# The written orders of a gated linear attention with an FFN behind it, laid out anew on all five queues of one core

## The chip, the cores and the metric

The kernel runs on one core of one Trainium2 chip. The core has a matrix engine (TensorE, PE in the rows of the profile), a vector engine (VectorE, DVE), an activation engine (ScalarE, ACT), a general engine (GpSimd, POOL) and a queue that issues transfers (SyncE, SP). Each takes its own instructions in the order in which they were written, and they meet only at semaphores. The metric is the time of one execution on the device in microseconds (us). The kernel before has a median of 187.74 us over three runs (187.13 to 188.03).

## The reference

Attention first: 4 batches, 8 heads, 768 steps, 48 channels a head, with a state of 48 x 48 for each head that decays by a gate for each channel.

```
f = 1 / (1 + exp(-f_logit))
for t in range(S):
    state = f[t][:, None] * state + outer(k[t], v[t])
    y[t]  = q[t] @ state
x   = y as 3072 tokens x 384
out = (relu(x @ w_gate) * (x @ w_val)) @ w_out        # 384 -> 1536 -> 384, float32
```

## The kernel before, in words

**Chunks.** The 768 steps are worked in windows of 128. A *unit* is two windows of one batch; there are 12 units (`seq`): units 0 to 3 are the first 256 steps of the four batches, 4 to 7 the next, 8 to 11 the last. The window w of unit u is 2u or 2u + 1. Each SBUF row holds two neighbouring steps (an even and an odd one).

**What a unit does** (`unit`, L525). It loads f, k, q and v (L468, 384 KB each, from SP). ACT makes `exp(-f)` (L546) and its logarithm `ln(1 + ..)`, into `bneg` in units 0 to 2 (L555), or in place with a sum of the two steps on another engine (L552, "sum") in the units behind. PE makes the running sums over a window with a triangular matrix (L562 to L564, into a PSUM bank called bc). ACT takes the exponentials of these with either sign (L577, L580, L587): `expo` in SBUF or in place in the bank. DVE and POOL multiply q and k by them: the *hats* (L599 for whole ones, L605 for halves). Units 0 to 3 transpose the hats on PE (L637, with a copy to `qkT`, L402 on ACT or L403 on DVE), the others by a transfer that SP issues (L648). PE multiplies k and q for the scores (L662); the causal mask is laid on by DVE straight from PSUM (L676) or by a copy on ACT (L671) and a product on POOL (L673): `ptm`. v is copied to `vpad` and `vrest` in pieces (L400, L402, L403). The decay of a window, `dec`, comes from a small matmul (L699, L703) and an exponential (L708), or from a row of `expo` by way of DRAM (`rates`, L683 and L692). PE sums k times v into a state (L717, L727); `new_state` (L506) adds the old state (`ssum`, L517, DVE) and multiplies by the decay (L520, POOL; L513 for the first). `out_of` (L740) makes a window's output from scores times v and q times the old state, transposed in place (L760) or plain (L767, L771) with a transposing transfer behind it (L790), into `xT`.

**The FFN.** Four windows make a group of 512 tokens, six groups. `ffn_hidden` (L799) does one of twelve slices of 128 hidden channels: three matmuls for the gate and three for the value (L811), a relu on ACT (L816), their product on DVE (L823, `gT`). Groups 0 and 1 work the first six slices in two halves of 256 tokens. `ffn_out` (L829) makes a window's output in four steps of three matmuls (L841), then a copy (L402 or L403, `osb`) and a store (L862).

**Weights.** POOL issues twelve transfers (L482), four slices of each matrix, which also convert to bf16. In POOL's queue they stand between its other work. Two of the loads are named as things that a slice must wait for, in the string `FIRST`.

**What sets the order.** Everything is recorded first as 1,088 operations with a running number, and the order on each engine is a written list of these numbers, `SEQUENCE` (from L184). `HOMES` says which PSUM tile lives in which of the eight banks, and in which order; a tile waits until the one before it in its bank has been read. `UNITS` names the engine for each copy, hat, mask product and sum (k0 is the hat of k at the even steps, tk the copy of k's transposes, m01 a mask product, v10 a piece of v, r0 and r1 its rest, x0 and o0 the copies of outputs). `FILLERS` puts matmuls on zeros (L892) ahead of some operations of PE at the start: after the first of its waits and before the others. `follow` (L85) takes the lists as they are, `needs` (L131) finds which semaphores an instruction has to wait for, and `run` (L904) writes each engine's stream. The estimated durations in the code choose nothing any more.

Some numbers that the text below uses: loads 37 to 40 are f, k, q, v of unit 0, 41 to 44 those of unit 1. On ACT 65, 66 are the exponential and the logarithm of unit 0, 103 and 104 those of unit 1, 69, 70, 73, 74 the exponentials of unit 0's sums. On POOL 53 to 60 are the slices wg0, wv0, wg1, wv1, wg2, wv2, wg3, wv3. On PE 154 is the first projection, 184 and 188 values of the second weight slice, 570 the running sum of unit 6. 588 and 589 are the transposing transfers of unit 6, 647 the rates of unit 7.

## Time and profile before

| | |
|---|---|
| median of three runs | 187.74 us (187.13 to 188.03) |
| profiled execution | 187.22 us, its span 186.0 us |
| TensorE busy | 179.1 us (96%) |
| VectorE, ScalarE, GpSimd busy | 123.1, 119.9, 103.4 us |
| data moved | 32.89 MB, mean 177 GB/s |

In the page, a line of the groups names the source line, the engine, the operation, the tiles as out<-in and the shapes, then the busy time and the mean duration of one, then the idle time ahead of it and what ended that. A line of the timeline begins with the start in us from the span's start and the length; "x3" is three instructions in a row, and what stands in square brackets is idle time ahead and what ended it. Matmuls overlap each other, so a row of PE shows a longer time than the pitch at which they follow. A line of the chain is a piece of the work that ended last. In the rows of the stages stand the stretch, its length, and for PE, weight loads, DVE, ACT and POOL the busy time and number of instructions, then the granted clock, the share of the DMA engines and GB/s. "DMA to landing" gives the shortest, the median and the longest time from the issue of a transfer to its landing, for the transfers asked for. "PEld" is the loading of weights into TensorE, which lies beside the matmuls; "SPq" and "POOLq" are the queues in which transfers are issued.

### The profile page before, as it was taken

How to read it: one execution, taken by the hardware profiler on the slowest of the kernel's cores; microseconds unless marked ns; L12 is line 12 of the kernel's file. 1: busy time of each engine (PE TensorE's matmuls, PEld its weight loads, DVE VectorE, ACT ScalarE, POOL GpSimd, SP SyncE). 2: the span in 40 equal slices, each digit the busy share in tenths (PEclk: the TensorE clock that was granted, in tenths of full speed). 3: DMA queues.
4: the chain of work that ended last, by engine and by line, in shares of the span. 5: the costliest groups of instructions: out<-in, count | busy, mean ns of one | idle time of the engine just before them, and what ended most of it. 6: DMA issues, size and time to landing. Idle time of an engine off the chain costs nothing.

```text
span 186.0 us, 4305 instructions
## 1 busy us (share of the span) xinstructions
PE 179.1 (96%) x1672; PEld 103.7 (56%) x1694; DVE 123.1 (66%) x235; ACT 119.9 (64%) x242; POOL 103.4 (56%) x137
## 2 busy tenths in 40 slices
PE   7888899999999999999999999999999999999995
PEld 2455486467577555545655554556545465445464
DVE  4289866799278989789669777785785352252531
ACT  3989796958987887988776563653664640444302
POOL 5179944999356789989829987540850550000000
DMA  5999999959899999899998898988034332110105
GB/s 152 325 325 285 231 204 206 266 96 175 173 305 180 238 314 263 206 186 217 251 243 214 237 227 194 201 135 226 4 74 124 97 85 76 42 46 0 42 0 212
DMA packets 83167, 32.89 MB, mean 177 GB/s; under 512 B 75334, under 2 KB 83148, under 8 KB 83148
## 3 DMA queue, kind: packets, MB, share of 16 engines
q1 hardware_dynamic: 78348, 29.09, 64.1%
q0 software_dynamic: 4800, 3.54, 12.7%
q8 instruction: 13, 0.21, 0.4%
q14 instruction: 6, 0.05, 0.1%
HBM read 25.96 MB, written 4.73 MB: 165 GB/s over the span
## 4 chain that ended last, share of the span: by engine, by line
PE 75%; POOL 7%; DMA 6%; SPq 4%; ACT 3%; DVE 2%; issue 2%; POOLq 0%; DVEq 0%
PE ps L811 44%; PE ps L841 21%; DMA q_in<-in_q_dram 6%; SPq L468 4%; PE ps L662 2%; POOL hats L605 2%; PE ps L771 1%; PE ps L637 1%; PE ps L760 1%; POOL ptm L673 1%; PE ps L767 1%; POOL hats L599 1%; POOL vpad L403 1%; POOL st L520 1%; PE ps L727 1%
## 5 line engine op out<-in xcount | busy, mean ns | idle before, releaser
L823 DVE TENSOR_TENSOR gT<-relu,ps 128x512 bf16<-128x512 bf16 (+1 forms) x84 | 49.7, 625 | 29.9 <-PE ps L811 28.7
L816 ACT ACTIVATE relu<-ps 128x512 bf16<-128x512 f32 (+1 forms) x84 | 43.1, 536 | 32.5 <-PE ps L811 21.6
L811 PE MATMUL ps<-xT,wg 128*128 128x512 bf16 (+1 forms) x242 | 53.9, 348 | 0.9 <-issue 0.3
L811 PE MATMUL ps<-xT,wv 128*128 128x512 bf16 (+1 forms) x243 | 53.6, 348 | 0.5 <-issue 0.2
L841 PE MATMUL ps<-wo,gT 128*128 128x384 bf16 (+2 forms) x300 | 52.2, 320 | 0.0
L841 PEld LDWEIGHTS ps<-wo,gT 128*128 128x128 bf16 x300 | 28.3, 98 | 18.5 <-ACT ptm L671 0.2
L811 PEld LDWEIGHTS ps<-xT,wg 128*128 128x128 bf16 x252 | 23.5, 98 | 20.1 <-DVE hats L599 0.4
L605 POOL TENSOR_TENSOR hats<-q_in,expo 64x384 bf16<-64x384 f32 x28 | 27.9, 995 | 11.7 <-ACT expo L580 8.3
L811 PEld LDWEIGHTS ps<-xT,wv 128*128 128x128 bf16 x252 | 23.4, 98 | 19.2 <-DVE gT L823 0.4
L673 POOL TENSOR_TENSOR ptm<-ptm,seen 128x512 bf16<-128x512 bf16 x21 | 23.9, 1156 | 16.3 <-ACT ptm L671 16.1
L605 DVE TENSOR_TENSOR hats<-k_in,ps 64x384 bf16<-64x384 f32 x32 | 17.6, 551 | 5.8 <-ACT osb L402 2.4
L676 DVE TENSOR_TENSOR ptm<-ps,seen 128x512 bf16<-128x512 f32 x27 | 17.5, 685 | 3.2 <-PE ps L662 3.0
L671 ACT ACTIVATE ptm<-ps 128x512 bf16<-128x512 f32 x21 | 12.1, 608 | 7.4 <-PE ps L662 7.2
L520 POOL TENSOR_TENSOR st<-ssum,dec 128x384 bf16<-128x384 f32 x16 | 13.2, 830 | 3.3 <-DVE ssum L517 2.4
L402 ACT ACTIVATE osb<-ps 128x384 f32<-128x384 f32 x17 | 8.3, 487 | 6.7 <-PE ps L841 5.0
L580 ACT ACTIVATE expo<-ps 128x384 f32<-128x384 f32 x22 | 10.2, 496 | 2.6 <-DVE ps L569 2.6
L403 POOL CAST vpad<-v_in 64x384 bf16<-64x384 f32 x22 | 11.0, 500 | 1.3
L546 ACT ACTIVATE f_in<-f_in 128x768 f32<-128x768 f32 x12 | 10.1, 846 | 2.4 <-DMA f_in<-in_f_logit_dram 2.3
L517 DVE TENSOR_TENSOR ssum<-ps,st 128x384 f32<-128x384 f32 x16 | 8.8, 554 | 4.0 <-PE ps L717 2.9
L552 POOL TENSOR_TENSOR bneg<-f_in 128x384 bf16<-128x384 f32 x8 | 8.0, 995 | 5.9 <-ACT f_in L550 5.7
L587 ACT ACTIVATE ps<-ps 128x384 f32<-128x384 f32 x22 | 10.6, 494 | 0.0
L892 PE MATMUL ps<-zeros 128*128 128x512 bf16 (+4 forms) x26 | 8.2, 448 | 0.3 <-DVE ptm L676 0.2
(90 smaller groups left out, 172.8 us busy)
## 6 DMA issues: line engine op xcount, KB each, us to landing
f_in<-in_f_logit_dram SPq DMA_DIRECT2D x12, 384.0 KB, 4.5
v_in<-in_v_dram SPq DMA_DIRECT2D x12, 384.0 KB, 4.9
k_in<-in_k_dram SPq DMA_DIRECT2D x12, 384.0 KB, 5.8
q_in<-in_q_dram SPq DMA_DIRECT2D x12, 384.0 KB, 5.0
out_dram<-osb SPq DMA_DIRECT2D x22, 192.0 KB, 2.1
wg<-in_moe_w_gate_dram POOLq DMA_DIRECT2D x4, 288.0 KB, 8.1
wv<-in_moe_w_val_dram POOLq DMA_DIRECT2D x4, 288.0 KB, 9.7
wo<-in_moe_w_out_dram POOLq DMA_DIRECT2D x4, 288.0 KB, 6.0
```

Of the source, the lines that this page charges most:

```text
L403: return engine[e].tensor_copy(out, src)
L520: add(e, lambda: engine[e].tensor_tensor(t4(s_new), t4(tmp), rate, ALU.mult), [key] + dk, [f"S{b}_{y}"], **(dict(occ=0.79, lat=0.1) if e = ...
L580: add("ACT", lambda: sc.activation(expo[:, ei, i, 0, :], bc[i].ap[:, 0:HD], AF.Exp, scale=-1.0), [bc[i]], [f"expq{ei}_{i}"], **act_t(HD))
L587: add("ACT", lambda i=i, ex=ex: sc.activation(bc[i].ap[:, 0:HD] if in_place else ex[:, 1, :], bc[i].ap[:, 0:HD], AF.Exp, scale=1.0), [bc[i ...
L605: op = add(e, lambda i=i, n=n, x=x, e=e, y=y, lo=lo, exps=exps: engine[e].tensor_tensor(hats[64 * i:64 * i + 64, hi, y, x, :, 0:D], by_i[n ...
L671: add("ACT", lambda pt=pt, s=sj[j]: sc.activation(pt, s.ap[:, :].rearrange("p (n t) -> p n t", n=NP), AF.Copy), [sj[j]], [f"raw{mis[y]}_{j ...
L673: add("POOL", lambda pt=pt, mask=mask: gp.tensor_tensor(pt, pt, mask, ALU.mult), [f"raw{mis[y]}_{j}", "seen"], [f"raw{mis[y]}_{j}", f"ptm{ ...
L676: add("DVE", lambda pt=pt, mask=mask, s=sj[j]: ve.tensor_tensor(pt, s.ap[:, :].rearrange("p (n t) -> p n t", n=NP), mask, ALU.mult), [sj[j ...
L811: mm = te.matmul(bank.ap[:, 0:n], wt[:, kt, j * 128:(j + 1) * 128], xT[xi][:, kt, n0:n1], start=(kt == 0), stop=(kt == NK - 1))
L816: add("ACT", lambda: sc.activation(relu[ri][:, n0:n1], gate.ap[:, 0:n], AF.Relu), [gate], rk, **act_t(n))
L823: return ve.tensor_tensor(o, a, b, ALU.mult)
L841: mm = te.matmul(bank.ap[:, 0:cut[1] - cut[0]], gT[gi][:, j, r * C:(r + 1) * C], wo[:, j, cut[0]:cut[1]], start=(j == 0), stop=(j == NJ - 1))
```

## The change

All operations stay as they are, with the same numbers. What changes is the five lists in `SEQUENCE`, the banks in `HOMES`, the places of the fillers, the engines of 65 operations in `UNITS`, and the loads that the weight slices wait for in `FIRST`. In SP's list unit 0's q becomes the third load and v of unit 1 the ninth. In ACT's list the four exponentials of unit 0's sums (74, 70, 69, 73) stand ahead of unit 1's logarithm (104). Of unit 0, the even hat of k goes to POOL and the odd one to DVE, and the copy of k's transposes from ACT to DVE. The profile's line numbers of the kernel after are larger by one from `FILLERS` on.

```diff
 SEQUENCE = {
     "PE": [
-        36, 68, 67, 132, 106, 105, 93, 83, 85, 90, 121, 87, 123, 95, 96, 125, 128, 99, 244, 135, 134, 245, 138, 154, 146, 178, 174, 150, 170,
...
+        36, 68, 67, 85, 106, 83, 105, 87, 123, 90, 121, 132, 128, 125, 93, 244, 95, 134, 96, 99, 245, 135, 138, 154, 146, 150, 174, 262, 170,
+        148, 152, 172, 178, 156, 176, 260, 180, 190, 186, 182, 166, 184, 162, 164, 158, 168, 268, 264, 188, 160, 198, 273, 192, 202, 194, 290,
...
     "ACT": [
-        65, 66, 103, 104, 69, 73, 74, 70, 94, 10, 133, 107, 108, 111, 112, 84, 81, 79, 80, 78, 124, 242, 243, 97, 130, 120, 246, 247, 100, 250,
...
+        65, 66, 103, 74, 70, 69, 73, 104, 10, 111, 78, 107, 108, 112, 124, 242, 116, 243, 133, 79, 115, 130, 94, 246, 247, 97, 100, 250, 136,
...
     "DVE": [
-        22, 17, 18, 14, 19, 15, 16, 28, 24, 26, 25, 2, 23, 11, 12, 13, 5, 117, 71, 27, 72, 76, 86, 113, 109, 92, 122, 91, 89, 88, 98, 101, 127,
...
+        22, 11, 27, 23, 14, 26, 25, 24, 15, 12, 17, 2, 18, 5, 76, 72, 28, 75, 86, 84, 82, 89, 113, 13, 109, 19, 88, 92, 16, 122, 91, 129, 127,
...
     "POOL": [
-        30, 33, 6, 20, 21, 8, 3, 9, 32, 35, 34, 4, 0, 1, 7, 75, 110, 53, 116, 31, 77, 114, 82, 118, 54, 119, 55, 115, 56, 131, 57, 58, 102, 141,
...
+        0, 30, 8, 33, 31, 6, 9, 7, 20, 21, 1, 3, 4, 71, 114, 110, 53, 80, 32, 77, 54, 117, 81, 120, 118, 119, 55, 131, 56, 57, 58, 141, 59, 34,
...
     "SP": [
-        37, 41, 44, 38, 39, 43, 42, 40, 45, 47, 46, 49, 48, 50, 51, 52, 142, 283, 323, 143, 144, 145, 284, 285, 425, 424, 286, 329, 471, 470,
...
+        37, 41, 39, 38, 43, 40, 42, 45, 44, 47, 46, 49, 48, 50, 51, 52, 283, 142, 323, 143, 144, 284, 285, 286, 145, 424, 425, 329, 445, 471,
...
-FILLERS = {68: (9, 0, 448), 132: (3, 0, 256), 83: (2, 0, 320), 85: (1, 0, 0), 90: (5, 0, 384), 123: (1, 0, 0), 96: (2, 0, 0), 134: (2, 6, 0)}
+FILLERS = {68: (9, 0, 448), 85: (6, 0, 192), 106: (0, 0, 512), 87: (2, 0, 0), 123: (4, 1, 384), 132: (1, 1, 0), 128: (1, 2, 0), 95: (1, 0, 0)}
...
-FIRST = 'f0 k0 q0 v0 f1 k1 q1 v1 f2 k2 q2 v2 f3 k3 q3 v3 wg0@q0 wv0 wg1 wv1@f1 wg2@k0 wv2@k2 wg3@q1 wv3 wo0@k3 wo1@q0 wo2@q1 wo3'
+FIRST = 'f0 k0 q0 v0 f1 k1 q1 v1 f2 k2 q2 v2 f3 k3 q3 v3 wg0@f0 wv0@f1 wg1@f0 wv1@k1 wg2@k0 wv2@k0 wg3@v1 wv3@f0 wo0@v0 wo1@k2 wo2@f2 wo3@q3'
```

The banks and engines follow in the same way: `HOMES` has eight new rows, and in `UNITS` for instance unit 0 goes from `'tk': 'ACT', 'r1': 'ACT', 'v11': 'POOL', 'v10': 'ACT', 'k0': 'DVE', 'k1': 'POOL'` to `'tk': 'DVE', 'r1': 'POOL', 'v11': 'DVE1', 'v10': 'POOL', 'k0': 'POOL', 'k1': 'DVE'`.

More of the change, by code (lines that the diff above doesn't have):

```diff
@@ new lines @@
+    7: {'v10': 'POOL', 'kps': True, 'q1': 'POOL', 'v01': 'ACT', 'q11': 'POOL', 'm00': 'DVE', 'v11': 'ACT', 'even': 'DVE', 'm10': 'POOL', 'm11': 'DVE', 'm01': 'POOL', 'q10': 'POOL', 'qps': False, 'q01': 'POOL', 'q0': 'POOL', 'o0': 'ACT', 'x1': 'DVE', 'td': True, 'x0': 'ACT', 'o1': 'ACT', 'v00': 'POOL', 'sum': 'POOL'},
+    8: {'m10': 'DVE', 'v11': 'ACT', 'q01': 'POOL', 'm01': 'POOL', 'even': 'DVE', 'q0': 'POOL', 'v10': 'DVE1', 'q1': 'POOL', 'm00': 'DVE', 'kps': True, 'q11': 'POOL', 'q00': 'POOL', 'qps': False, 'v00': 'DVE1', 'q10': 'POOL', 'v01': 'ACT', 'pr': False, 'td': True, 'x0': 'ACT', 'o1': 'DVE', 'x1': 'DVE', 'o0': 'ACT', 'sum': 'POOL'},
@@ L274 @@
+    11: {'q0': 'DVE', 'v01': 'ACT', 'q10': 'POOL', 'm00': 'DVE', 'q01': 'POOL', 'm11': 'POOL', 'q1': 'POOL', 'q00': 'POOL', 'kps': True, 'v11': 'POOL', 'm01': 'DVE', 'q11': 'POOL', 'even': 'DVE', 'v00': 'POOL', 'm10': 'POOL', 'v10': 'ACT', 'yy': True, 'o1': 'DVE', 'td': True, 'x0': 'ACT', 'x1': 'ACT', 'o0': 'DVE', 'sum': 'DVE'},
 }
 SLICES = {'wg': [3, 3, 3, 3], 'wv': [3, 3, 3, 3], 'wo': [3, 3, 3, 3]}
[L276 removed]
+FIRST = 'f0 k0 q0 v0 f1 k1 q1 v1 f2 k2 q2 v2 f3 k3 q3 v3 wg0@f0 wv0@f1 wg1@f0 wv1@k1 wg2@k0 wv2@k0 wg3@v1 wv3@f0 wo0@v0 wo1@k2 wo2@f2 wo3@q3'
```

46 lines of the change are left out of this document (21 added, 25 removed), and 81 rows, old and new, of tables (SEQUENCE, UNITS).

## The prediction

> **What bounds the kernel now.** I read the page's busy shares and slices first, then the stages, then TensorE's own waits, and last the chain.
>
> ```profile
> PE 179.1 (96%) x1672; PEld 103.7 (56%) x1694; DVE 123.1 (66%) x235; ACT 119.9 (64%) x242; POOL 103.4 (56%) x137
> ...
> PE   7888899999999999999999999999999999999995
> ...
> DMA  5999999959899999899998898988034332110105
> ```
> ```profile
> 20.00:40.00 20.00, 19.55 (x241) 13.03 (x246) 15.01 (x32) 14.84 (x35) 14.32 (x19) 1.00 1.10 209
> ...
> 60.00:80.00 20.00, 19.74 (x249) 11.20 (x251) 17.50 (x33) 17.18 (x35) 17.78 (x21) 1.00 1.03 253
> ```
> ```profile
> PE ps L811 <- issue: 0.5, 3, 0.2
> PE ps L811 <- DVE ssum L517: 0.2, 1, 0.2
> ```
> The last two rows are all the waits of TensorE (PE) between 24 and 184 us: 0.7 us in 160. From 24 us on the kernel is a gapless stream of matmuls, so a new order cannot make that part shorter by more than 0.7 us; it can only put holes into it. What can be gained lies ahead of 24 us, where units 0 and 1 run as a chain over all engines:
>
> ```profile
> 4.42 4.84 DMA q_in<-in_q_dram
> ...
> 15.28 1.02 ACT qkT L402
> ...
> 18.87 0.53 ACT vpad L402
> ...
> 20.00 0.57 DVE st L513
> ...
> 20.86 0.55 PE ps L760 x25
> 21.41 2.42 PE ps L811 x18
> ...
> 24.73 2.29 PE ps L811 x21
> ...
> 176.71 7.36 PE ps L841 x57
> ...
> 184.09 0.29 DVE osb L403
> ```
> The chain waits for unit 0's q until 9.26 us, then works through hats, transposes, scores, states and outputs, and reaches the first projections at 21.4. Twenty-one matmuls of 256 columns take 2.29 us, 0.109 each; the first eighteen took 2.32 (21.35 to 23.67 by the row below) where 1.96 would do: 0.36 us went into waits for banks and xT.
>
> **The change at the start, step by step.** The rows that I use for the walk, ACT, DVE, POOL and PE in turn:
>
> ```profile
> 6.05 0.83 ACT L546 ACTIVATE f_in<-f_in 128x768 f32<-128x768 f32 x1
> 6.91 0.84 ACT L555 ACTIVATE bneg<-f_in 128x768 bf16<-128x768 f32 x1
> 7.66 0.85 ACT L587 ACTIVATE expo<-ps 128x384 f32<-128x384 f32 x2
> 8.40 0.87 ACT L580 ACTIVATE expo<-ps 128x384 f32<-128x384 f32 x2
> ...
> 11.32 1.03 ACT L402 ACTIVATE qkT<-ps 128x1024 bf16<-128x1024 bf16 x1
> ```
> ```profile
> 11.19 0.69 DVE L403 COPY qkT<-ps 128x1024 bf16<-128x1024 bf16 x1 [0.71 <-PE ps L637]
> 11.80 1.01 DVE L599 TENSOR_TENSOR hats<-k_in,ps 128x384 bf16<-128x384 f32 x2
> ...
> 14.14 1.88 DVE L676 TENSOR_TENSOR ptm<-ps,seen 128x512 bf16<-128x512 f32 x3
> ...
> 20.59 0.56 DVE L517 TENSOR_TENSOR ssum<-ps,st 128x384 f32<-128x384 f32 x1
> ```
> ```profile
> 8.60 1.00 POOL L599 TENSOR_TENSOR hats<-k_in,expo 128x384 bf16<-128x384 f32 x1 [5.07 <-ACT expo L587]
> ...
> 13.12 0.50 POOL L403 CAST vpad<-v_in 64x384 bf16<-64x384 f32 x1
> ...
> 18.22 0.78 POOL L482 DMA_DIRECT2D wv<-in_moe_w_val_dram  x1
> 19.02 1.17 POOL L673 TENSOR_TENSOR ptm<-ptm,seen 128x512 bf16<-128x512 bf16 x1
> ```
> ```profile
> 12.49 0.40 PE L662 MATMUL ps<-qkT 48*128 48x128 bf16 x8
> ...
> 21.35 2.49 PE L811 MATMUL ps<-xT,wg 128*128 128x256 bf16 x18
> 23.67 0.50 PE L637 MATMUL ps<-ident,hats 128*128 128x128 bf16 x6
> ```
> ```profile
> DMA to landing us min/median/max: 4.8/4.9/4.9
> ```
> The last row holds for the six loads that SP issues from 1.93 to 8.00; they follow each other by 1.2 us. *q0 becomes the third load instead of the fifth*: it lands at about 6.8 instead of 9.26, k0 stays fourth, v0 moves up to sixth (10.5) and v1 falls back to ninth (14.1).
>
> *ACT's four exponentials of unit 0 pass unit 1's logarithm (0.84).* The first starts at 6.91, right behind unit 1's exponential, and all four (0.37 apart) are done at 8.5 instead of 9.27: 0.75 sooner. The logarithm ends at 9.24 instead of 7.75: unit 1's cumulative sums come 1.5 later. What waited for the logarithm: the two sums of unit 1 on PE, then unit 1's four exponentials, which end at 12.3 instead of 11.4.
>
> *Hats and transposes of unit 0.* q hats on DVE (0.55 each) from 7.44; POOL makes the first k hat (1.00) from 8.17 to 9.17, DVE the second until 9.2. PE's transposes of k then stand behind unit 1's first sum in PE's order and start at 9.6. DVE copies k's transpose (0.69) where ACT did (1.03): done at 10.96, and the first scores start at 11.0 instead of 12.49: 1.5 sooner.
>
> *Unit 1 becomes the late one.* Its q hats on POOL need the later exponentials: two at 1.00 end at 12.6; PE transposes q until 13.3, ACT copies (1.02) until 14.4. DVE, in order: a v copy, mask product, two k hats (waiting for ACT until 12.3), two mask products, the copy of k's transpose, done at 15.4. Scores of unit 1 at 15.4 and 15.7 instead of 16.6: still 1.2 sooner.
>
> *States and outputs.* ACT now holds a queue behind that copy: exponential and logarithm of unit 2 (0.84 each), two dec, four v copies of 0.52, one raw mask copy; it comes to the dec of unit 0 at 18.35. DVE's first state product waits for that, so 18.4 to 18.95, output two of unit 0 at 19.0, then state and sum of unit 1 (0.55 each) to 20.0, its outputs at 20.05 and 20.3. POOL has a weight issue (0.78) ahead of the last mask product (1.17): 19.05 to 20.25, just ahead of the output that needs it. The last output takes 0.55 (the chain's 20.86 row), so the first projection starts at **20.9 instead of 21.35: -0.45**. Behind it I find one wait: a group needs a bank that ACT's copy of unit 2's q transpose holds until 24.1, 0.15. Of the 0.36 lost there before, **0.2 is won**.
>
> **Weights.** POOL issues them in order, so each moves with what stands ahead: wg slice 0 at 12.6 (before 11.52), wv 0 at 14.8 (15.65), wg 1 at 18.25 (16.95), wv 1 at 20.2 (18.22). The row that matters:
>
> ```profile
> DMA to landing us min/median/max: 9.1/9.1/9.1
> ```
> ```profile
> 28.27 0.82 PE L811 MATMUL ps<-xT,wv 128*128 128x256 bf16 x6
> ```
> wv 1 took 9.1 us and landed at 27.3, 0.95 before its first use at 28.27. After the change its first use comes 0.28 of PE work earlier in the order, and 0.65 earlier by the start: 27.3. If the time to landing is mostly queue behind wg 1, which in both orders starts at about 21, it lands at 27.3 to 27.5 again; if all of the 9.1 follows the issue, at 29.3. First bound 0, second +2.1 us. I take **+0.1**, since of the four issues up to 19 us the first took 5.3 and this one 9.1 for the same bytes: 3.8 of it is queue.
>
> ```profile
> DMA to landing us min/median/max: 5.3/6.5/9.1
> ```
> The Trainium skill, page "DMA: Bandwidth & Descriptors", section on queues, rings and completion order, says that each DMA engine takes packets round-robin from the queues that hold work. By that rule the weight queue keeps its share whatever the issue times, and the sum would stand at +0.1; the rows of 5.3 and 9.1 agree, but no row of before shows wv 1 issued behind a shorter queue.
>
> **The dense part.** 65 copies, mask products and sums change engine, net four fewer on POOL and four more on ACT; DVE, ACT and POOL are each under 18 of 20 us busy in the stage that has most, so the loads fit and only order can hurt. I compared, for every wait of PE in 24 to 184, how much PE work lies between the matmul that starts the chain and the one that needs its result. Chains of one copy need about 0.3 more than the copy; the new order has 12 with under 0.55 to spare, the old 27, and those cost it 0.7 in all. I leave 0.7 in place: **0**. The two places with least cover: POOL at 52 to 68 us (below), and unit 6's DMA transposes, which SP now issues behind unit 7's rates and which by my walk land at 82 for a use at 82.8. Stores moved late on SP (windows 10, 12, 15) free their buffers 4 us or more ahead of the next writer. The tail keeps its order from the last window on: 0. The fillers are 13,824 columns instead of 14,208, all in waits: 0. Should that cover be gone, a filler that ran past its wait would cost its own 0.2.
>
> **Sum**, against the profiled execution's own 187.22 us (span 186.0): -0.45 - 0.2 + 0.1 = **-0.55, 186.7 us**. That execution stands 0.5 below the median of 187.74, inside the three runs (187.13 to 188.03). 0.5%, 0.9 us, is about what can be told from no change here.
>
> **Rivals.**
> 1. *wv 1 is late* (slower). Price +2.1 as above, less 0.65, and each later slice in POOL's queue (0.6 to 2 later) keeps it: 188.6. It decides once wv 1 lands after 28.0. For: slack was only 0.95 and the issue is 2.0 later. Against: the queue reading.
> 2. *POOL holds units 4 to 6* (slower).
> ```profile
> 67.28 0.99 POOL L552 TENSOR_TENSOR bneg<-f_in 128x384 bf16<-128x384 f32 x1
> ```
> ```profile
> 69.53 0.33 PE L562 MATMUL ps<-bneg,upto 128*128 128x384 bf16 x1
> ```
> Unit 6's sum ended 1.26 before PE used it. The new order puts a state product (0.82) among the q hats of unit 4 and ahead of this; my walk leaves 0.7. If two more POOL steps of 1.0 come late, PE stands 1.3: 187.9, and with a second such place 189.
> 3. *Nothing is gained*: the start is held by the outputs of unit 1 as before (its logarithm is 1.5 later), and the new order brings unit 1's last output at 20.9 rather than 20.3: 187.2.
> 4. *More is gained*: the 0.36 and half of the 0.7 go, and queues behind ACT run shorter than my walk: 185.9.
> 5. *PE falls to half rate at the start.*
> ```profile
> 1.66 4.01 PE L892 MATMUL ps<-zeros 128*128 128x512 bf16 x10
> ```
> Ten fillers in 4.0 us, 0.43 apart (the last a shorter one), where 512 columns take 0.216 later (the 0.109 for 256, doubled). If that rate returned for as long as this row lasts, the projections under it would end 2.0 later: 187.22 - 0.65 + 0.1 + 2.0 = 188.7. By my walk PE's longest hole at the start is about 1 us (13.9 to 15.4, with a filler in it), so I give it little. The Trainium skill, page "TensorE: Matmul & The Clock Gate", part 1, gives half rate after an idle window of about 3.4 us; by that figure the price would be an estimated 1.7, and no hole in the walk is long enough for it.
>
> **How the numbers follow.** Forecast 0.42 (186.0 to 187.4: 0.28 of it faster by over 0.5%, 0.14 within); more gained 0.16 (faster); nothing gained 0.11 (within); wv 1 late 0.15, POOL 0.13, half rate 0.03 (slower, at the median's scale from 188.7 on; 0.01 of them within). Faster 0.44, same 0.26, slower 0.30. The likeliest alone spans 186.0 to 187.4; the range for 8 in 10 reaches from the larger gain to the slower cases: 185.8 to 189.2.
>
> **What would show it.** In the trace after: q_in third on SP and landed near 6.8; four expo activations from 6.9 to 8.5 ahead of the second bneg; first scores near 11.0, unit 1's near 15.4; first projection near 20.9; wv's second slice issued near 20.2 and landed before 27.5; TensorE's waits after 24 us again under 1 us. Wrong if PE waits for a DMA of wv at 27 us, for bneg near 69 us, for qkT near 83, or if the first projection is not before 21.3.

## The result: 1% slower, and the profile after

The changed kernel takes 189.8 us (median of 189.14 to 190.24) where the kernel before takes 187.88 beside it: 1.0101 of it, 95% interval 1.0057 to 1.0146, or 1.9 us slower. The forecast was 186.7, in a range that ended at 189.2. The profiled execution of the changed kernel took 190.16 us (span 188.9), which is near the upper end of its runs; a difference between the two traces (2.9 us at the end) is therefore larger than the difference of the medians, and sums below are made from ratios where they can be. The ratios come from several chips, and their intervals are wide beside the differences that are taken of them. Every line number of the changed kernel is one higher than before.

The page of the changed kernel: busy time, the slices of TensorE and of the DMA engines, and the shares of the chain.

```profile
PE 181.8 (96%) x1693; PEld 103.4 (55%) x1693; DVE 124.7 (66%) x235; ACT 122.6 (65%) x246; POOL 100.9 (53%) x133
...
PE   7997899999999999999999999999999999999995
...
DMA  5999999919999999997899999795242124201204
...
PE 49%; DMA 17%; SPq 9%; POOL 9%; DVE 5%; issue 5%; ACT 4%; POOLq 0%; ACTq 0%
```

The last row says that something is new: DMA and SP's sequencer (SPq) hold 26% of the chain that ended last. The same row of the kernel before gives them 10%, and TensorE 75%:

```profile
PE 75%; POOL 7%; DMA 6%; SPq 4%; ACT 3%; DVE 2%; issue 2%; POOLq 0%; DVEq 0%
```

The waits of TensorE in the changed kernel from 20 us on (line waited in, what ended the wait, us in total, times, longest; gaps under 0.15 us are not listed; "issue" is idle time in which the engine waits for nothing that the profile shows):

```profile
PE ps L761 <- issue: 0.8, 1, 0.8
PE ps L812 <- DMA wv<-in_moe_w_val_dram: 0.5, 1, 0.5
PE ps L768 <- POOL st L521: 0.3, 1, 0.3
PE ps L663 <- issue: 0.2, 1, 0.2
PE ps L812 <- DMA xT<-xn: 0.2, 1, 0.2
PE ps L812 <- ACT osb L403: 0.2, 1, 0.2
```

Three groups are to be explained: 0.8 us on "issue", 0.5 for the second slice of wv, and several waits of 0.2 to 0.3. The start itself went nearly as walked, up to the middle of unit 1's last output. The changed kernel's timeline (start, duration, engine, line, shapes, idle time before it), ACT and then TensorE:

```profile
6.66 0.85 ACT L581 ACTIVATE expo<-ps 128x384 f32<-128x384 f32 x2
7.40 0.87 ACT L588 ACTIVATE expo<-ps 128x384 f32<-128x384 f32 x2
8.14 0.86 ACT L556 ACTIVATE bneg<-f_in 128x768 bf16<-128x768 f32 x1
```
```profile
11.01 0.40 PE L663 MATMUL ps<-qkT 48*128 48x128 bf16 x8
...
15.77 0.62 PE L663 MATMUL ps<-qkT 48*128 48x128 bf16 x16
...
20.27 0.28 PE L761 MATMUL ps<-qkT,st 128*32 128x128 bf16 x6
21.34 0.29 PE L761 MATMUL ps<-qkT,st 128*32 128x128 bf16 x6 [0.79 <-issue]
21.41 0.44 PE L761 MATMUL ps<-ptm,vpad 128*32 128x128 bf16 x16
21.78 0.94 PE L812 MATMUL ps<-xT,wg 128*128 128x256 bf16 x7
```

Unit 1's last output began at 20.27. Then TensorE stood for 0.79 us in the middle of twelve equal matmuls that wait for nothing, so the first projection came at 21.78: later than before (21.35). From there on the kernel lost 2.5 us more against the kernel before in these two executions, in some eight places (28.6, 51.9, 61.3, 63.4, 69.6, 90.4, 103.9 and 127.2 us).

### The profile page after: what moved, and what is told of

It is laid out like the page before. It is cut to its first block, busy times and chain, and to the rows that moved or that the text cites. A ratio compares the mean times of both kernels' runs of the same rounds, so it can differ in the third digit from the quotient of the medians.

```text
span 188.9 us, 4339 instructions
## 1 busy us (share of the span) xinstructions
PE 181.8 (96%) x1693; PEld 103.4 (55%) x1693; DVE 124.7 (66%) x235; ACT 122.6 (65%) x246; POOL 100.9 (53%) x133
## 4 chain that ended last, share of the span: by engine, by line
PE 49%; DMA 17%; SPq 9%; POOL 9%; DVE 5%; issue 5%; ACT 4%; POOLq 0%; ACTq 0%
PE ps L812 28%; PE ps L842 15%; DMA v_in<-in_v_dram 8%; SPq L469 6%; DMA wv<-in_moe_w_val_dram 4%; DMA qkT<-hats 2%; POOL vpad L404 2%; POOL hats L606 2%; DMA xT<-xn 2%; SPq L791 2%; PE ps L663 2%; DVE gT L824 2%; ACT relu L817 1%; DVE hats L606 1%; PE ps L761 1%
## 5 line engine op out<-in xcount | busy, mean ns | idle before, releaser
L824 DVE TENSOR_TENSOR gT<-relu,ps 128x512 bf16<-128x512 bf16 (+1 forms) x84 | 50.4, 625 | 23.5 <-PE ps L812 16.6
L817 ACT ACTIVATE relu<-ps 128x512 bf16<-128x512 f32 (+1 forms) x84 | 43.6, 536 | 32.8 <-PE ps L812 26.6
L812 PE MATMUL ps<-xT,wv 128*128 128x512 bf16 (+1 forms) x252 | 56.7, 349 | 0.8 <-DMA wv<-in_moe_w_val_dram 0.5
L812 PE MATMUL ps<-xT,wg 128*128 128x512 bf16 (+1 forms) x252 | 55.9, 349 | 0.1
L842 PE MATMUL ps<-wo,gT 128*128 128x384 bf16 (+2 forms) x300 | 53.7, 320 | 0.0
L812 PEld LDWEIGHTS ps<-xT,wg 128*128 128x128 bf16 x252 | 23.2, 98 | 19.3 <-ACT f_in L551 0.5
L581 ACT ACTIVATE expo<-ps 128x384 f32<-128x384 f32 x22 | 10.3, 489 | 6.0 <-DVE ps L570 5.6
L403 ACT ACTIVATE osb<-ps 128x384 f32<-128x384 f32 x14 | 6.8, 494 | 8.9 <-PE ps L842 8.5
L404 DVE COPY osb<-ps 128x384 f32<-128x384 f32 (+2 forms) x11 | 5.6, 520 | 10.2 <-PE ps L842 10.2
L553 POOL TENSOR_TENSOR bneg<-f_in 128x384 bf16<-128x384 f32 x6 | 6.0, 998 | 10.3 <-ACT f_in L551 10.0
L403 ACT ACTIVATE vpad<-v_in 64x384 bf16<-64x384 f32 x19 | 9.9, 521 | 1.1 <-DMA v_in<-in_v_dram 0.8
```

The costliest lines, as they stand in the source:

```text
L403: return sc.activation(out, src, AF.Copy)
L812: mm = te.matmul(bank.ap[:, 0:n], wt[:, kt, j * 128:(j + 1) * 128], xT[xi][:, kt, n0:n1], start=(kt == 0), stop=(kt == NK - 1))
L817: add("ACT", lambda: sc.activation(relu[ri][:, n0:n1], gate.ap[:, 0:n], AF.Relu), [gate], rk, **act_t(n))
L824: return ve.tensor_tensor(o, a, b, ALU.mult)
L842: mm = te.matmul(bank.ap[:, 0:cut[1] - cut[0]], gT[gi][:, j, r * C:(r + 1) * C], wo[:, j, cut[0]:cut[1]], start=(j == 0), stop=(j == NJ - 1))
```

## Experiments

Theory A: TensorE ran out of instructions at 20.5 us. Theory B: in the stretch up to 105 us, where the DMA slices read 9 nearly throughout, transposes and loads land later than in the kernel before, and TensorE has no room for it. Rivals: an operand that the profile does not name (for A); the written orders themselves (for B).

### 1. Where does the loss sit: the start, or what follows?

Two hybrids. h1 has the kernel before's rows up to the first projections (all five queues, with units 0 and 1, fillers and first loads), the changed rows behind; h2 the other way round. In the ACT row of h2, for example:

```diff
+        65, 66, 103, 74, 70, 69, 73, 104, 10, 111,
...
+        100, 250, 136, 139,   # changed row up to here
+        251, 155, 175, 179, 151, 147, 171,   # row of the kernel before
...
```

> The kernel before for units 0 and 1 (all five queues up to the first projections, SP's first 18 issues, the fillers), the changed kernel's orders behind that. Theory 'dense part': the holes behind 40 us come along, 1.8 to 2.3 us over the kernel before: 189.7 to 190.2 where that stands at 187.9. Rival 'the start': what the changed kernel loses it loses ahead of 30 us (0.44 at the first projection, 0.64 at wv's second slice); the time is within 0.4 of the kernel before.

> The changed kernel for units 0 and 1, the kernel before's orders behind that. Theory 'dense part': 0.4 to 1.1 us over the kernel before (0.44 at the first projection, wv's second slice late, some of it taken back): 188.3 to 189.0 where that stands at 187.9. Rival 'the start': as slow as the changed kernel, 189.4 to 190.2.

Measured: h1 189.25 us, 1.0109 (1.0083 to 1.0134) of the kernel before; h2 188.14 us, 1.0041 (1.0022 to 1.0059). Both halves cost something, the later one more. The first projection of h2 came at 22.07, 0.72 later than in the kernel before, and that is nearly all of its 0.0041 (0.77 us). h1 is no clean share: where the two orders meet it waits 0.5 for unit 2's hats and 0.3 for an xT copy, waits that neither parent has. In h2 the stop on issue is back, 0.9 long, at 20.75.

### 2. Instruction supply

A queue of the page named "instruction" moves 13 packets of 16,384 bytes. In the trace of the changed kernel its first packet begins at 19.15 us and takes 0.96; TensorE resumes 1.23 us after its end. In the kernel before the first packet begins at 18.48 and takes 0.93. Unit 1's last output begins there at 20.61, on DVE's state product (done at 20.56), and its fourth matmul starts 0.24 behind the third, at 20.86, 1.45 after the packet's end: apparently a small stop of the same kind, whose greater part lay under the wait for DVE. The DMA view of the changed kernel for 19.1 to 20.2 us shows the packet:

```profile
q8 instruction: 1, 0.02, 5.5%
```

When it stopped, TensorE had run 449 instructions that the trace records (221 matmuls, 221 weight loads and seven of its sequencer), called records below; the expectations name the one that came next, the 450th. If that is a packet's boundary, then more records ahead of it must move the stop. The fillers were cut into more and smaller matmuls of the same columns:

```diff
-                    for _ in range(count):
-                        warm(banks[k])
-                    if rest:
-                        warm(banks[k], rest)
+                    left = count * WARM + rest
+                    while left > 0:
+                        warm(banks[k], min(left, 120))
+                        left -= 120
```

> The changed kernel with its fillers cut into pieces of 120 columns (the same columns, some 90 matmuls more before 19 us). Theory 'instruction fetch': TensorE stopped at 20.55 for 0.79 us at its 450th record because the 16,384-byte packet on the queue named instruction, which came once 381 records had run (at 19.15 us), had landed only at 20.11. With some 176 records more ahead of it that packet comes near 16 us, the hole at 20.5 goes (or shrinks under 0.2), and the first projection starts at 20.9 to 21.1 instead of 21.78. The time moves by no more than 0.4, since the second slice of wv still lands at 28.4 and TensorE then waits for it longer. Rival 'a late operand that the profile does not name': the hole stays at 20.5 with 0.7 to 0.9 us.

Measured: 188.88 us, 1.0084 (1.0061 to 1.0107). The stop at 20.5 is gone, and another one has appeared:

```profile
21.78 0.71 PE L812 MATMUL ps<-xT,wg 128*128 128x256 bf16 x5
23.54 0.61 PE L638 MATMUL ps<-ident,hats 128*128 128x128 bf16 x8 [1.05 <-issue]
```

This stop stands behind 705 records, 256 more than 449, and ends 1.27 us after a packet that began at 21.31 and took 0.96. So the boundary stayed in the instruction stream, 256 records of 64 bytes being 16,384 bytes (the 64 is worked out from the two, not shown). In h2, a_half, a_sp and a_sp2 the stop stands behind 449 records again, and h1 has one of 0.2 there. The expectation that this run would hold no stop had missed the second boundary. The 256 records ahead of the stop at 20.5 had run in 4.8 us, those ahead of the second one in 4.4. With pieces of 180 columns the boundaries fall where 256 records take longer (7.4 and 7.0 us, measured in a_f180):

```diff
-                        warm(banks[k], min(left, 120))
-                        left -= 120
+                        warm(banks[k], min(left, 180))
+                        left -= 180
```

> The changed kernel with its fillers cut into pieces of 180 columns and nothing else. Theory 'instruction fetch': no hole on issue over 0.25 us, the first projection at 20.8 to 21.1 as in the run with the early weight slice, but unit 2's sums not late (there they once waited 1.62 us for f of unit 2 and the granted clock then fell to 0.53), and every execution at a clock of 1.0; wv's second slice again lands at 28.2 to 28.5, so TensorE waits there 0.8 to 1.3 us and most of the 0.8 us is given back: 1.007 to 1.010 of the kernel before. Rival 'what is won at the start stays won': 1.003 to 1.006.

Measured: 188.63 us, 1.0045 (1.0010 to 1.0081). The output runs through, and the first projection starts at 20.75, 0.6 ahead of the kernel before:

```profile
20.25 0.34 PE L761 MATMUL ps<-qkT,st 128*32 128x128 bf16 x12
20.42 0.40 PE L761 MATMUL ps<-ptm,vpad 128*32 128x128 bf16 x16
20.75 0.72 PE L812 MATMUL ps<-xT,wg 128*128 128x256 bf16 x5
```

The first projection starts 1.03 earlier than in the changed kernel: theory A is shown, and the rival (an unnamed late operand) falls. By the ratios 0.0056 of 187.9, 1.05 us, went with the edit, but the two intervals overlap (1.0010 to 1.0081 and 1.0057 to 1.0146), so that size is rough. Not all was given back to the weights (wv's second slice landed at 27.52, the wait for it was 0.6), so the expectation of 1.007 to 1.010 was too high.

> The kernel before with its fillers cut into pieces of 180 columns. Theory 'instruction fetch': unit 1's last output started there at 20.61, 1.20 us after its packet had landed at 19.41, but DVE's state sum was done only at 20.56, so taking the fetch away gains at most 0.05: 0.998 to 1.002 (a null test). Rival 'small fillers themselves make TensorE faster or slower': outside that.

Measured: 189.22 us, 1.0085 (1.0054 to 1.0116), with the same edit on the kernel before. This was meant as a null test, and its expectation (0.998 to 1.002) failed. The first projection came at 20.93, 0.42 sooner, and yet the kernel became slower. The trace is that of its fastest execution, 188.09 us, so it shows about half of the loss. Its TensorE waits behind 40 us:

```profile
PE ps L662 <- ACT ptm L671: 0.8, 1, 0.8
PE ps L811 <- issue: 0.3, 2, 0.2
PE ps L811 <- DVE ssum L517: 0.2, 1, 0.2
```

The wait of 0.8 stands at 86.1 us, at unit 7's scores. The profile names ACT, whose mask copy was done at 85.35; the second transpose of unit 7's q and k landed at 86.62 and TensorE went on at 86.91. In the kernel before it landed at 85.62. It took 3.2 us in both; SP issued it at 83.44 instead of 82.38. So an earlier start did not carry through here. Part 5 returns to this wait.

Cutting the fillers is not a change of TensorE alone, though. There are 14 instruction packets instead of 13, and all come at other times: the first begins at 13.43 in b_f180 and 13.64 in a_f180, in the kernel before and the changed one at 18.48 and 19.15. The load of unit 2's q is issued at 10.2 to 10.3 in all four. It lands at 15.30 in the kernel before and 15.18 in the changed one, but at 16.34 in b_f180 and 16.56 in a_f180. The time to landing in the changed kernel and in a_f180:

```profile
DMA to landing us min/median/max: 5.0/5.0/5.0
```
```profile
DMA to landing us min/median/max: 6.3/6.3/6.3
```

In a_fetch, where the packet begins at 12.05, the load before it (unit 1's v, issued at 9.13) is late already: 15.40 instead of 13.96. In h2, a_half and a_sp, with the packet at 19.0 to 19.3, both loads land within 0.2 of the changed kernel. So a packet that comes while loads are in flight goes with landings 1.0 to 1.4 later, and SP's next loads are then issued later too (from 1 to 3 us later in b_f180 between 14 and 30 us). This is a rival for the loss of b_f180, moved packets rather than the earlier start, and no run tells the two apart.

### 3. The head of the weight queue

POOL issues the first slice of wg at 12.40 instead of 11.52, and the others follow it. The issues in the changed kernel's timeline, the first four of eight:

```profile
12.40 0.93 POOL L483 DMA_DIRECT2D wg<-in_moe_w_gate_dram  x1
14.56 0.78 POOL L483 DMA_DIRECT2D wv<-in_moe_w_val_dram  x1
18.08 0.78 POOL L483 DMA_DIRECT2D wg<-in_moe_w_gate_dram  x1
20.04 0.80 POOL L483 DMA_DIRECT2D wv<-in_moe_w_val_dram  x1
```

They landed at 17.92, 22.49, 25.61 and 28.46; before, at 16.84, 21.43, 24.24 and 27.29. All four are 1.1 to 1.4 later, whatever their own issue times were (wv 0 was issued 1.1 earlier than before and landed 1.1 later). Two places were tried for the first issue, with the fillers in pieces of 180 columns:

```diff
-  ... 4, 71, 114, 110, 53, 80, ...
+  ... 4, 71, 53, 114, 110, 80, ...      # a_start, h2_best: issue at 9.1
+  ... 4, 71, 114, 53, 110, 80, ...      # a_f180w, h2_f180w: issue at 11.2
```

> The changed kernel with its fillers cut into pieces of 180 columns (some 55 matmuls more ahead of 17 us, so that the 256-record steps at which TensorE stopped, records 450 and 705, fall at what were records 340 and 595, where 256 records take 8 us), and with the first weight slice issued by POOL ahead of unit 1's q hats (at 9.1 instead of 12.4 us). Theory 'instruction fetch and the head of the weight queue': no hole on issue over 0.25 us, first projection at 20.9 to 21.1, wv's second slice lands before 27.5 and its hole (0.48 at 28.1) goes; the time falls by 0.8 to 1.2 us, to 1.003 to 1.006 of the kernel before. Rival 'the weights follow their own issue': wv's second slice lands at 28.2 or later and the hole grows to over 1 us, 1.008 to 1.011. Second rival, 'the early weight slice takes the loads' turn': q and k of unit 1 land 0.5 us or more later and the first projection is not before 21.4.

> The changed kernel's start with the same two repairs (fillers in pieces of 180 columns, first weight slice early), the kernel before's orders behind it. Theory: the start is worth the 0.45 us that was forecast once TensorE does not stop for its instructions, and the dense part of the kernel before keeps it: first projection at 20.9 to 21.1 and 0.996 to 0.999 of the kernel before. Rival 'the dense part of the kernel before is cut to its own start': new holes of 0.3 to 0.6 us behind 40 us take it back, 1.000 to 1.004.

Measured: a_start 1.0072 (1.0033 to 1.0111), with ten executions from 187.93 to 192.22 us (median 190.16) at granted clocks from 1.00 down to 0.98; h2_best 190.28 us, 1.0179 (1.0114 to 1.0244). In h2_best unit 2's sums on TensorE waited for a late logarithm:

```profile
18.27 0.50 PE L565 MATMUL ps<-bneg,upto 128*128 128x384 bf16 x1 [1.62 <-ACT bneg L557]
```

and the granted clock (the third number from the right in the answer by stretches) fell behind that wait:

```profile
16.00:18.00 2.00, 0.65 (x21) 0.41 (x15) 2.00 (x4) 1.15 (x2) 1.00 (x2) 1.00 1.22 264
18.00:20.00 2.00, 1.73 (x21) 1.14 (x23) 0.01 (x1) 2.00 (x8) 1.87 (x4) 0.53 1.22 257
20.00:22.00 2.00, 2.00 (x69) 1.74 (x64) 1.57 (x3) 0.88 (x3) 1.93 (x3) 0.62 1.00 257
```

What made the logarithm late stands ahead of it on ACT, a copy of unit 1's v (waits of ACT, 13 to 19 us):

```profile
ACT vpad L404 <- DMA v_in<-in_v_dram: 2.0, 1, 2.0
```

That v was issued at 8.99, as in the changed kernel (9.06), and landed at 16.82 instead of 13.96; unit 2's f landed on time (12.68), other than the later expectations say. In a_start the same v landed at 15.60. An issue at 9.1 is too early: the second rival of a_start's expectation (the weights take the loads' turn) fits, though it hit unit 1's v and not its q and k, and the moved instruction packet (at 14.74) may add to it.

> The changed kernel with fillers in pieces of 180 columns and the first weight slice issued ahead of POOL's second q hat of unit 1. Theory: the hole at wv's second slice goes from 0.56 to under 0.3 and the time to 1.001 to 1.004 of the kernel before. Rival: the gain is given back behind 40 us, 1.004 to 1.007; or unit 1 late by the q hat, 1.006 to 1.010.

> The same with the first weight slice issued ahead of POOL's second q hat of unit 1 (11.2 instead of 12.4 us; at 9.1 it once made f of unit 2 late). Theory 'the weight queue is set by its head': wv's second slice lands about 1 us sooner, 27.0 to 27.5 instead of 28.3, and its hole shrinks to under 0.4: 0.993 to 0.998. Rival: the q hat behind the issue comes 0.8 later and unit 1's scores with it, 1.000 to 1.004.

> The changed kernel's start with its fillers in pieces of 180 columns, the kernel before's orders behind it. Theory 'the start gains, the dense part loses': the first projection some 0.9 us earlier than in the kernel before (as in the run with the pieces alone), wv's second slice late by 0.6 to 0.8, the dense part as before: 186.9 to 187.7 where the kernel before has 187.7, 0.996 to 1.000. Rival 'no start can gain, because SP's and POOL's DMAs set the pace of the dense part': new waits for transposes at 69 to 105 us, 1.002 to 1.006.

Measured: a_f180w 188.09 us, 1.0026 (0.9997 to 1.0055), its wait for wv 0.3 instead of 0.6, as expected: the best of the repairs, 0.75% faster than the changed kernel by the ratios, and not told apart from the kernel before. h2_f180 189.11 us, 1.0071 (1.0043 to 1.0100), and h2_f180w 189.90 us, 1.0121 (1.0082 to 1.0160). The kernel before's later orders kept nothing of the better start: the first projection came at 21.06 in h2_f180, a wait of 0.4 for unit 2's hats followed at once, and the transpose of unit 7 cost 0.9 (h2_f180w: 1.8) at 87 us, the same place as in the kernel before with cut fillers.

In these runs the head of the queue is not what sets the later slices. a_f180 and a_f180w differ in the place of the first issue alone (12.38 and 11.13). The first slice landed 1.38 sooner in the second, wv's second slice only 0.16 sooner (27.36 for 27.52); in a_start, with the first issue at 9.06, it landed at 27.53. And the changed kernel and a_f180 issue all four slices at the same times within 0.02, yet in a_f180 the first lands 1.26 later and wv's second 0.94 sooner. So the wait for wv in a_f180w shrank half by the 0.16 and half by a first projection that came 0.13 later. Why all four slices are late in the changed kernel stays open.

### 4. SP's order

> The changed kernel with the kernel before's list for SP from the 19th issue on (the first 18 are the same set). Theory 'SP's order': the holes of TensorE in the changed kernel that end with a DMA transpose or a dec transfer (0.27 at 51.9 us, 0.43 at 69.6, 0.31 at 90.4, 0.33 at 103.9, 0.42 at 127.2) go, 1.3 to 1.8 us less than the changed kernel's 189.8: 188.0 to 188.5. Rival 'the engines' order': the transposes are late because ACT, DVE and POOL make their sources late; the time stays within 0.4 of 189.8 and the holes stay within 0.1 of their size.

```diff
-        ... 52, 283, 142, 323, 143, 144, 284, 285, 286, 145, 424, 425, ...
+        ... 52, 142, 283, 323, 143, 144, 145, 284, 285, 425, 424, 286, ...
```

Measured: 198.16 us, 1.0581 (1.0551 to 1.0611). The kernel before's list does not fit the other four queues. SP's waits between 50 and 66 us, of its own queue:

```profile
SPq L919 <- POOL hats L600: 3.0, 1, 3.0
SPq L649 <- POOL hats L606: 2.7, 1, 2.7
```

SP stood at transposes whose hats POOL made later in the new order, with a load of v queued behind them on SP. ACT waited for that load (its waits between 55 and 66 us), and TensorE 3.2 for the output copy that stood behind it on ACT:

```profile
ACT vpad L403 <- DMA v_in<-in_v_dram: 3.6, 1, 3.6
```

So SP's list of the one kernel does not go with the other four queues of the other.

> The changed kernel with five SP issues moved: one load of f (unit 7) behind the first transpose of unit 5, the loads of f (unit 11) and v (unit 8) behind the two transposes of unit 7's outputs, unit 8's rates and its first dec transfers ahead. Theory 'transposes stand behind queued loads': the holes of 0.43 at 69.6, 0.33 at 103.9 and 0.42 at 127.2 us go, and the transposes concerned land 3 to 4 us behind their issue instead of 4.7 to 5.9: 0.7 to 1.2 us less than the changed kernel, 1.004 to 1.007 of the kernel before where the changed kernel stands at 1.010. Rival 'their sources are late': the holes stay within 0.15 of their size, 1.008 to 1.011.

```diff
-  ... 329, 445, 471, 470, 490, ... 604, 781, 609, 493, 655, 660, 665, ... 815, 241, ... 769, 783, ...
+  ... 329, 471, 445, 470, 490, ... 604, 609, 655, 660, 781, 493, 665, ... 815, 769, 771, 241, ...
```

Measured: 193.69 us, 1.0334 (1.0277 to 1.0390). Up to 118 us the theory held: three transposes to xT that SP issues between 95 and 100 us land 2.6 us after their issue instead of 4.5, and TensorE is 1.7 us ahead of the changed kernel at that point. In that window, for the kernel before, the changed one and this one:

```profile
xT<-xn SPq DMA_TRANSPOSE x3, 3.2
```
```profile
xT<-xn SPq DMA_TRANSPOSE x3, 4.5
```
```profile
xT<-xn SPq DMA_TRANSPOSE x3, 2.6
```

Then SP waited for the rates transfer that had been moved ahead, and unit 8's transposes came 2.7 us later:

```profile
SPq L693 <- DMA rates<-expo: 2.5, 1, 2.5
```
```profile
121.73 1.03 PE L663 MATMUL ps<-qkT 48*128 48x128 bf16 x16 [3.18 <-DMA qkT<-hats]
```

The wait of 3.18 was followed by a granted clock of 0.50 in the stretches from 122 to 126 us.

> The changed kernel with three loads moved on SP and nothing else: f of unit 7 between the two transposes of unit 5, f of unit 11 and v of unit 8 behind unit 7's output transposes (the move of unit 8's rates, which held SP for 2.5 us in the run before, is left out). Theory 'transposes stand behind queued loads': unit 7's two transposes land 2.3 to 2.7 us after their issue instead of 5.9 and 3.9, the hole at 103.9 goes, the one at 69.6 falls under 0.3, 0.5 to 1.0 us less than the changed kernel: 1.005 to 1.008. Rival: the stream waits for the next late thing instead and stays at 1.009 to 1.011.

> Both of these repairs together. If the causes are separate they add, 1.3 to 1.8 us less than the changed kernel: 1.000 to 1.004 of the kernel before. If the weights' queue takes the start's part back: 1.004 to 1.007.

a_sp3 is a_sp2 without the move of 769 and 771; a_best2 adds the pieces of 180 columns. Measured: 190.89 us, 1.0126 (1.0051 to 1.0200), and 191.16 us, 1.0165 (1.0118 to 1.0212). In a_sp3 the three transposes land in 2.7 us (in a_best2, with the same order on SP, in 3.9), and it gains nothing: unit 8's rates store, behind the loads that were moved, is issued 1.2 us later on SP, and ACT must wait for it before it may write its exponentials (waits of ACT in a_sp3, 112.5 to 116 us):

```profile
ACT expo L581 <- DMA rates<-expo: 1.9, 1, 1.9
```

ACT's v copy follows 1.2 later and TensorE waits 0.7 for it at 117.8. In these runs, whatever went first on SP, the next thing was late.

### 5. Is it the traffic?

The last two runs leave every order as it is and take traffic away (line 465 of the changed kernel; the same line in the kernel before with pieces of 180 columns):

```diff
-        h0, h1 = {"": (0, H), "a": (0, NP), "b": (NP, H)}[part]
+        h0, h1 = {"": (0, H if u < 4 else NP), "a": (0, NP), "b": (NP, H)}[part]
```

> The changed kernel, but the loads of f, k, q and v of units 4 to 11 bring only heads 0 to 3 (heads 4 to 7 keep what an earlier unit left in the buffer, so the output is another), which takes 6.3 of the 32.9 MB away, nearly all of it between 22 and 110 us. All instructions and orders stay. Theory 'full DMA queues set the pace of the dense part': the holes that end with a transpose or a dec transfer (51.9, 69.6, 90.4, 103.9, 127.2 us) go or fall under 0.15, the transposes land 2.0 to 3.0 us after their issue, 1.4 to 2.0 us less than the changed kernel: 1.000 to 1.003 of the kernel before; what is left is the stop for instructions at 20.5. Rival 'the orders themselves': the holes stay, 1.008 to 1.011.

> The kernel before with fillers in pieces of 180 columns, whose first projection came 0.4 us earlier and whose end came 1.6 us later, with the same half loads (another output again). Theory 'full DMA queues': the hole of 0.82 us at 86.1 (transpose of unit 7) goes and the 0.4 us of the start reach the end: 0.993 to 0.999 of the kernel before. Rival 'an earlier start upsets the order of DVE and POOL': the hole stays, 1.005 to 1.009.

Measured: a_half 188.01 us, 1.0044 (1.0029 to 1.0059); b_f180_half 187.13 us, 0.9991 (0.9976 to 1.0006). The stretch of 60 to 80 us (its length, busy time of PE, PEld, DVE, ACT and POOL, then granted clock, DMA share, GB/s) in the changed kernel and in a_half:

```profile
60.00:80.00 20.00, 19.50 (x252) 10.82 (x250) 16.50 (x32) 17.60 (x37) 15.83 (x19) 1.00 1.14 261
```
```profile
60.00:80.00 20.00, 19.99 (x252) 11.12 (x249) 17.27 (x33) 17.73 (x37) 15.30 (x17) 1.00 0.59 136
```

With half of the DMA share the half microsecond of holes is gone. The waits of TensorE from 20 us on, in a_half and in b_f180_half:

```profile
PE ps L761 <- issue: 1.0, 1, 1.0
PE ps L812 <- DVE gT L824: 0.2, 1, 0.2
```
```profile
PE ps L760 <- DVE st L513: 0.2, 1, 0.2
```

The changed orders of all queues run without a wait that the profile lists behind 29 us once the DMA queues have room, and unit 7's wait in the kernel before with cut fillers falls from 0.8 to 0.13. There the transpose took longer than in b_f180 (4.8 us against 3.2), but SP issued it 2.3 us sooner: what moved with the traffic here is the issue. Theory B is shown for these holes, with the same instructions and orders and less traffic; a price of the orders by themselves is not seen. The amount was expected too high (1.4 to 2.0 us less than the changed kernel): it is 0.0057, 1.1 us, by the ratios, whose intervals just touch, and the stop for instructions, which is left in, was 1.0 here instead of 0.8. With half of the loads the changed kernel stands 0.88 us behind the kernel before with cut fillers (188.01 and 187.13), which is less than its stop.

Two things stay open. The kernel before as it is was not run with half of the loads, so how much less traffic would give it is not known. And the holes are not fixed by orders and traffic alone: the profiled execution of a_f180, its fastest at 187.91 us, has the whole traffic and the same orders (with cut fillers), and of the places behind 50 us it has a remnant of one (61.8, as in a_half) and a new one of 0.57 at 118.4; its slowest execution took 190.50.

The two shares, 1.05 for instructions and 1.1 for late landings, make 2.1 against a loss of 1.9. Both taken away at once was not run in the changed kernel, so that they add up is not shown.

### 6. The named move alone

> The kernel before with only the part that the change is named for: ACT's four exponentials of unit 0 ahead of unit 1's logarithm, unit 1's sums on TensorE behind unit 0's transposes, and SP's first 18 issues as in the changed kernel (q of unit 0 third). Theory 'unit 1 becomes the late one': the first scores come at 11.2 to 12.0 instead of 12.49, unit 1's scores not earlier than before, the first projection within 0.4 of 21.35, and the time within 0.4% of the kernel before. Rival 'the named order carries the gain': first projection 0.4 or more earlier, 0.996 to 0.998.

> The kernel before with the named move alone (ACT's exponentials of unit 0 ahead of unit 1's logarithm, unit 1's sums on TensorE behind unit 0's transposes, q of unit 0 third on SP), and with the three steps moved that would otherwise block a queue: DVE's and POOL's first copies of unit 1's v behind work that does not need that later load, ACT's copy of unit 0's k transpose ahead of unit 1's exponentials. Theory 'unit 1 becomes the late one': first scores at 10.6 to 11.5 instead of 12.49, but unit 1's last output not earlier and the first projection within 0.5 of 21.35; 0.997 to 1.005. Rival 'the named move is what gains': first projection at 20.9 or earlier and 0.996 or less. Rival 'the named move is what loses': first projection at 22 or later, 1.005 or more.

```diff
-        65, 66, 103, 104, 69, 73, 74, 70, 94, 10, 133, ...
+        65, 66, 103, 69, 73, 74, 70, 104, 94, 10, 133, ...
```

Measured: b_named 197.01 us, 1.0519 (1.0489 to 1.0549); b_named2 191.22 us, 1.0186 (1.0125 to 1.0248). In b_named TensorE stood 7.4 us at the transposes of unit 0, because DVE's row begins with a copy of unit 1's v, whose load had moved from third to ninth; its expectation (within 0.4%) failed on that block. In b_named2, with the three steps moved that block a queue, it still waited:

```profile
9.82 0.62 PE L639 MATMUL ps<-ident,hats 128*128 128x128 bf16 x8 [2.18 <-POOL hats L601]
```

and the first projection came at 24.27. Of the three outcomes named for b_named2 the last one came, that the move loses: alone, with so few followers, it does. That the changed kernel's start gains from the new engines of unit 0's hats and copies is argued from this, not isolated.

## Why the prediction was wrong, step by step

- **Loads, exponentials, hats, unit 0's scores: right.** Forecast 6.9 to 8.5 for the exponentials and 11.0 for the scores; measured 6.66 to 8.27 and 11.01.
- **Unit 1's scores at 15.4: 15.77.** The walk left out a setup fill of DVE that the new order puts behind a mask product; TensorE waited 0.43 for it (15.04). It cost nothing at the end: the last output began at 20.27, forecast 20.3.
- **"Of the 0.36 lost there before, 0.2 is won": right.** Between 21.78 and the wait for wv at 28.1 no hole of 0.1 us stands in the changed kernel's row of matmuls.
- **"The first projection starts at 20.9": 21.78. This step failed.** All operands were there; the instructions were not. In a_f180, where they were, it came at 20.75. The walk counted what each engine does and never asked whether TensorE's instructions arrive: some 170 records run in the 2.3 us ahead of the stop, since the small matmuls of units 0 and 1 stand close together there. Worth about 1 us: 1.03 in the traces, 1.05 by the ratios.
- **"wv 1: +0.1": 0.5 of waiting at 28.1.** The step that failed is that wg 1 starts "in both orders" at about 21: wv 0, the slice ahead of it, landed at 22.49 instead of 21.43, wg 1 at 25.61 instead of 24.24, and wv 1 followed it after 2.85 (before 3.05), as a queue would. Why the slices ahead were late stays open (part 3). It landed at 28.46, past the 28.0 at which the first rival was to decide; the price was a quarter of the 2.1 given, and in part it was hidden by the stop before it. The Trainium skill, page "DMA: Bandwidth & Descriptors", section on queues, rings and completion order, has each DMA engine take packets round-robin from its queues; by that rule +0.1 was argued. No run here isolates the share; in a_f180, with the same issue times as in the changed kernel, the four slices moved by -0.94 to +1.26.
- **"The dense part: 0": about 1.1 us by the ratios.** This step failed too. For copies and products the count of TensorE work between cause and use was right enough: no such wait over 0.15 is left behind 29 us in a_half. It went wrong for transposes and loads, for which the sum has no term: three transposes took 3.2 us at 95 to 100 in the kernel before and take 4.5 in the new order. That from 24 us on the kernel is "a gapless stream of matmuls" was true of the kernel before; the DMA row of 9s quoted beside it was the second bound, and the prediction made nothing of it. The 0.7 us that it "left in place" were not even waits: the trace of before lacks 19 records of the projections (485 where the changed kernel has 504), and each of the four waits that were counted is what one missing matmul (0.22) adds to the usual pitch at its place. The rows of b_f180 on "issue" and on ssum above are the same.
- **The rivals.** Nothing gained and more gained: no, the first projection lost 0.43. wv 1 late: in part. POOL in units 4 to 6: no wait of TensorE for it there; unit 6's transposes, the other place of least cover, were not late either; those of units 5 and 7 were (they landed at 69.5 and 90.4 for uses 0.1 later). Half rate at the start: not in the changed kernel, but in h2_best, by the mechanism described.

## What to carry to other kernels

A gapless TensorE does not mean that TensorE alone is the bound: read the DMA row of the slices beside it, and where both stand at 9, treat the time to landing as a thing that an order changes, not as a constant. Before moving many small matmuls together, count TensorE's instructions in steps of 256. In these kernels, with the DMA queues full, steps of 4.4 to 4.8 us ended in a stop of 0.8 to 1.05, and those of 6.2 us and more in one of about 0.2 (h1, kernel before) or in none. Cutting fillers shifts the steps at no cost in columns, but it shifts the instruction packets as well, and in a_fetch, a_f180 and b_f180 loads in flight at a packet landed 1.0 to 1.4 us later. An order of one queue taken from another version, or a move "alone", is a different kernel: in a_sp and in b_named a queue held a step that only the old neighbours could feed.

## What the hardware showed that was not expected

- TensorE stops between two matmuls without any wait when its next 16,384 bytes of instructions have not landed: 0.79 to 1.05 us in seven of the kernels (1.05 in a_fetch, 1.02 in a_half), ended 1.2 to 1.6 us after the packet's end, in six of them behind 449 records or 256 later. What sets the moment at which the packet is asked for stays open: it came after 381 records here, after 253 and 687 in a_fetch.
- The same packets go with late loads: q of unit 2 took 6.3 us to land in a_f180 and 5.0 in the changed kernel, issued at the same time. That the packet holds them up is argued from four kernels, not isolated.
- A wait of 1.62 us, with TensorE already busy only part of the time before it, was enough for a granted clock of 0.53 in the next 2 us (in the 3.41 us ahead of the fall, at 18.11, it had been busy for 1.60), and one of 3.18 us for 0.50 over 4 us. The Trainium skill, page "TensorE: Matmul & The Clock Gate", Part 1, speaks of an idle window of about 3.4 us that runs freely; the first case shows that TensorE need not be idle for all of it.
- The same three transposes land after 2.6 and 2.7 us in a_sp2 and a_sp3, where loads stand behind them, and after 4.5 in the changed kernel, where they stand behind loads; in a_best2, with the order of a_sp3, they took 3.9.
